# One written order for all engines, one inverse for two chunks and merged key-query products in a delta-rule attention with a softplus feed-forward layer

## The chip, the cores and the metric

One Trainium2 chip, one of its cores, one launch. The metric is the device time of the launch in microseconds (us); the kernel before was run three times: 306.86, 308.31 and 309.32 us, median 308.31 us. One further execution was profiled; every duration below comes from it.

In the profile PE is TensorE (matrix multiply; PEld is its weight load), DVE is VectorE, ACT is ScalarE, POOL is GpSimd and SP is SyncE, which here only issues DMAs.

## The reference, cut to what matters

Batch 4, 8 heads, 768 time steps, head size 48. The attention keeps one 48x48 state for each of the 32 (batch, head) pairs; its output feeds a two-layer network with softplus between.

```python
k_n = k / (np.linalg.norm(k, axis=-1, keepdims=True) + 1e-06)
for t in range(S):
    readout = np.einsum('bhd,bhde->bhe', q[:, :, t], state)
    y[:, :, t] = g[:, :, t] * readout
    v_old = np.einsum('bhde,bhd->bhe', state, kt)
    state = state + bt[:, :, :, None] * np.einsum('bhd,bhe->bhde', kt, vt - v_old)
...
h = x @ w_in                                            # 3072 x 384 by 384 x 2048
g = np.maximum(h, 0.0) + np.log1p(np.exp(-np.abs(h)))   # softplus
return (g @ w_out).astype(np.float32)                   # by 2048 x 384
```

Each state depends on the one before it. The kernel gets rid of the loop over t by chunks of 64 steps: within a chunk the updates solve a triangular system, whose inverse it computes for all heads at once; between chunks the state is carried.

## The kernel before, in words

**Tiling.** Time is cut into 12 chunks of 64 steps. A tile has 128 partitions: 64 time steps of two batches. All 12 chunks pass through the same items (the names are those of the code's `add` calls):

- `load` (line 344): k, q, v, g of a chunk, two DMAs of 192 KB for each, all issued on SP in one chain. `wload` (line 371): eight DMAs for the two weight matrices, issued on POOL.
- `front` (line 468): `cast` k and q to fp16; `trs`, 16 PE transposes (line 485); `kev`, copies from PSUM; `gramk`, 64 matmuls of the keys with themselves (lines 522 and 527); `kkc`, their negated copies into `kk`; `gramq`, 32 matmuls of keys with queries (line 561); `mask` (line 571).
- `norms` and `lane_beta` (lines 410 and 455): `ksq` (ACT), `red` (DVE), the root (ACT for the first chunks, `pow` on POOL later, line 443), `eps`, and `lbeta`.
- `inverse` (line 584): `ln`, a DVE transpose that brings each 32x32 block into one partition (line 591); `diag`, `prep` and 15 `step`s of two instructions each (lines 622 and 629), a forward substitution on 16x16 blocks; transposes back, `tn` and `t32` (lines 647 and 663), which land in fp32 tiles and are rearranged and cast by ACT (lines 654 and 670); then PE products that join the 16 blocks to 32 and prepare 64: `xmm`, `tmm` and `zmm`, with the copies `xs`, `td2` and `z`.
- `chain` (line 765), the part that carries the state: `ks` (keys by state), `w` (v minus it), `umm` (64 matmuls of 32x32 for a chunk, line 840), `u1`, `zu`, `u2`, `smm` and `s` (the new state), `qs` and `ymm` (readout), `y` (times g), `ytr` and `xt` (transposes for the network). `vs` scales v by the key norm on POOL (line 808).
- `dense` (line 998), the network: `g1` (line 1014), `soft` (softplus on ACT, line 1028), `g2` (line 1044), `o` (eviction) and `store`. Chunks 0, 1, 10 and 11 are done alone, with 256 columns in a `g1` matmul, the others in pairs, with 512.

**Two chunks in one inverse.** The lanes of a tile hold 32 blocks of two chunks. Chunks 0 and 1 have an inverse each, chunk 0 on DVE and chunk 1 on POOL; the other five inverses take two chunks each and run on POOL: seven in all.

**What sets the order.** Each item gets an engine and a priority from a table of words (`_TABLE`, line 1108). `Plan.run` (line 86) places the items by estimated costs: on each engine, among the items that are ready, the one with the lowest priority. That gives each engine a fixed program when the kernel is built. Among its costs is one for PE's instructions: `BLOCK` 128 matmuls and `FETCH` 3.5 (lines 49 and 50).

**Buffers.** Every tile comes from a ring of buffers: five PSUM banks for all small products (`d`), two for `g1` (`h`), one for `g2` (`o`); k has 3 buffers, q 2, v and g 4 each.

**Start.** DVE clears the padding of `kn` and `qn` (line 238). POOL issues the eight loads of beta, and clears `kk`, `nv` and `tt` (lines 272 and 275).

Of the kernel before, what the change touches and what calls it, by code (L numbers as in the profile page):

```python
# [16 lines left out]
class Ring:  # L17

    def __init__(self, tiles, ordered=True):
        self.free = [(0.0, i) for i in range(len(tiles))]
        self.tiles = tiles
        self.ordered = ordered
        self.made = self.given = 0


class Buf:
    def __init__(self, ring):
        self.ring = ring  # L30
        self.users = 0
        self.ap = None
        self.slot = None
        self.done = 0.0
        self.no = ring.made
        ring.made += 1


class Item:
    __slots__ = (  # L40
        "eng", "kind", "cost", "fn", "deps", "bufs", "prio", "start", "end", "tail", "n",
        "order", "mm", "mode", "leave", "dma", "after", "tag", "alt",
    )


class Plan:


    BLOCK = 128
    FETCH = 3.5  # L50
    HOP = 0.08
    SWITCH = 0.1
    STAY = 15
    LOOK = 0.15

    def __init__(self):
        self.items = []
        self.tag = None

    def add(  # L60
        self, eng, kind, cost, fn, deps=(), bufs=(), prio=0, tail=None, order=(), mm=0,
        mode=None, leave=None, dma=0.0, after=0.0, alt=None,
    ):
        it = Item()
        it.eng, it.kind, it.cost, it.fn = eng, kind, cost, fn
        it.deps = [d for d in deps if d is not None]
        it.order = [d for d in order if d is not None]
        it.bufs, it.prio = list(bufs), prio
        it.tail = (0.17 if eng == "PE" else 0.0) if tail is None else tail
        it.start = it.end = None  # L70
        it.n = len(self.items)
        it.mm, it.mode, it.leave, it.dma, it.after = mm, mode, leave or mode, dma, after
        it.tag, it.alt = self.tag, alt
        for b in it.bufs:
            b.users += 1
        self.items.append(it)
        return it

    def use(self, table):

        for it, word in zip(self.items, table.split()):
            en = {"P": "PE", "D": "DVE", "A": "ACT", "G": "POOL", "S": "SP"}[word[0]]
            it.cost = it.alt[en] if it.alt else it.cost
            it.eng, it.prio = en, int(word[1:])

    def run(self):
        left = {e: [] for e in ("PE", "ACT", "DVE", "POOL", "SP")}
        for it in self.items:
            left[it.eng].append(it)
        free = {e: 0.0 for e in left}  # L90
        pipe = 0.0
        mode = None
        issued, arrive = 0, [0.0, 0.0]
        done = []
        while any(left.values()):
            best = None
            for e, lst in left.items():
                cands = []
                for it in lst:
                    if any(d.end is None for d in it.order) or any(  # L100
                        d.end is None for d in it.deps
                    ):
                        continue
                    ready = it.after
                    for d in it.deps:
                        t = d.end + (d.tail + self.HOP if d.eng != e else 0.0)
                        ready = max(ready, t)
                    need = {}
                    for b in it.bufs:
                        if b.ap is None:  # L110
                            need[b.ring] = need.get(b.ring, 0) + 1
                    ok = True
                    for r, n in need.items():
                        if n > len(r.free) or (
                            r.ordered
                            and any(
                                b.no >= r.given + n
                                for b in it.bufs
                                if b.ring is r and b.ap is None
                            )  # L120
                        ):
                            ok = False
                            break
                        ready = max(ready, sorted(r.free)[n - 1][0])
                    if ok:
                        cands.append((ready, it))
                if not cands:
                    continue
                t0 = max(free[e], min(r for r, _ in cands))
                at = {it.n: max(t0, r) for r, it in cands}  # L130
                can = [it for r, it in cands if r <= t0 + self.LOOK]
                if e == "PE":

                    def late(it):
                        last = (issued + it.mm - 1) // self.BLOCK
                        at = arrive[min(last, len(arrive) - 1)]
                        return max(0.0, at - t0 - it.cost)

                    stall = min(late(it) for it in can)
                    can = [it for it in can if late(it) <= stall + 0.3]  # L140
                if e == "PE":
                    it = min(can, key=lambda x: (x.prio - self.STAY * (x.mode == mode), x.n))
                else:
                    it = min(can, key=lambda x: (x.prio, x.n))
                t0 = at[it.n]
                if best is None or t0 < best[0]:
                    best = (t0, e, it)
            if best is None:
                raise RuntimeError("no item can be placed")
            t0, e, it = best  # L150
            left[e].remove(it)
            for b in it.bufs:
                if b.ap is None:
                    b.ring.free.sort()
                    b.slot = b.ring.free.pop(0)[1]
                    b.ap = b.ring.tiles[b.slot]
                    b.ring.given += 1
            it.fn(it.eng) if it.alt else it.fn()
            it.start = t0
            if it.dma:  # L160
                free[e] = t0 + it.cost if e == "POOL" else max(t0 + it.cost, pipe - 4.0)
                pipe = max(pipe, t0 + it.cost) + it.dma
                it.end = pipe + 1.9
            elif e == "PE":
                if it.mode != mode:
                    t0 += self.SWITCH
                mode = it.leave
                end = t0 + it.cost
                block = issued // self.BLOCK
                issued += it.mm  # L170
                while issued // self.BLOCK > block:
                    block += 1
                    end = max(end, arrive[block])
                    arrive.append(end + self.FETCH)
# [1037 lines left out]
```

## Time and profile before

| | |
|---|---|
| median of three runs (lowest to highest) | 308.31 us (306.86 to 309.32) |
| profiled execution: span from first to last instruction | 307.5 us |
| PE busy, matmuls | 236.3 us, 6768 |
| DVE, ACT and POOL busy | 158.9, 142.9 and 142.6 us |
| first `g1` | 72.83 us after the start |
| first `g1` of 512 columns, that is of chunks 2 and 3 | 121.33 us |
| last matmul ends | 303.3 us |
| mean granted TensorE clock | 0.967 of full speed |

The profiled execution's own span lies 0.8 us under the median. Busy times of the engines overlap, since all run at once; a matmul's duration in a group is also longer than what it adds, since matmuls are pipelined. "issue" is time in which an engine waited for nothing that the profile shows. The strips of the page cut the span into 40 slices of 7.7 us, and each digit is a tenth.

### The profile page before, as it was taken

The numbers are of one execution on the slowest core, as the hardware profiler recorded it, in microseconds if no ns is written. First come the engines' busy times: TensorE is split into PE (matmuls) and PEld (weight loads), VectorE is DVE, ScalarE is ACT, GpSimd is POOL, SyncE is SP. The second block draws the span as 40 slices with busy tenths as digits, with TensorE's granted clock in tenths as the row PEclk, the third lists the DMA queues.
The fourth block names the chain that finished last, engine by engine and source line by source line (L and its number), as shares of the span: only waits on it lengthen the run. The fifth ranks groups of instructions, "written<-read, shape, count | busy, mean of one in ns | idle before, by whom it ended". The sixth has DMA issues, their size and how long they took to land.

```text
span 307.5 us, 14779 instructions
## 1 busy us (share of the span) xinstructions
PE 236.3 (77%) x6768; PEld 155.8 (51%) x6768; DVE 158.9 (52%) x306; ACT 142.9 (46%) x240; POOL 142.6 (46%) x262
## 2 busy tenths in 40 slices
PE   0130183277988997899987999959999899999993
PEld 0120163255756765455664556636555555567761
DVE  1189998442757786854873474645436611152000
ACT  3070086022754656726654674352656516715531
POOL 8916578557138887457761747811087000000000
PEclk9999999999999999969997999987999979999999
DMA  8999439999015979699298430843000111021122
GB/s 115 158 179 173 57 54 191 186 170 152 7 31 100 157 140 158 113 162 148 51 164 147 83 57 15 125 99 79 6 5 15 43 28 30 2 55 28 27 53 51
DMA packets 107711, 27.79 MB, mean 90 GB/s; under 512 B 100865, under 2 KB 107649, under 8 KB 107649
## 3 DMA queue, kind: packets, MB, share of 16 engines
q1 hardware_dynamic: 103680, 23.60, 47.5%
q0 software_dynamic: 3968, 3.25, 7.1%
q8 instruction: 53, 0.87, 1.2%
q14 instruction: 10, 0.07, 0.1%
HBM read 25.26 MB, written 4.72 MB: 98 GB/s over the span
## 4 chain that ended last, share of the span: by engine, by line
PE 61%; DVE 12%; issue 11%; POOL 11%; ACT 4%; POOLq 0%; ACTq 0%
PE h L1014 19%; PE o L1044 18%; PE d L485 3%; POOL tt L629 3%; POOL tmp L622 3%; PE d L684 2%; PE d L786 2%; DVE tt L629 2%; PE d L840 2%; PE d L939 2%; DVE tmp L622 2%; PE d L711 2%; DVE ln L591 2%; PE d L561 2%; PE d L877 2%
## 5 line engine op out<-in xcount | busy, mean ns | idle before, releaser
L1044 PE MATMUL o<-w_out,ga 128*128 128x384 f16 x384 | 77.9, 343 | 3.2 <-issue 1.9
L1028 ACT ACTIVATE ga<-h 128x512 f16<-128x512 f32 x96 | 57.2, 599 | 48.0 <-PE h L1014 45.4
L1014 PE MATMUL h<-xt,w_in 128*128 128x512 f16 (+1 forms) x384 | 74.8, 336 | 1.0 <-issue 1.0
L1044 PEld LDWEIGHTS <-ga 128*128 128x128 f16 x384 | 35.7, 101 | 26.1 <-issue 7.3
L1014 PEld LDWEIGHTS <-w_in 128*128 128x128 f16 x384 | 36.1, 100 | 21.7 <-issue 3.4
L629 POOL TENSOR_TENSOR tt<-tt,tmp 128x30 f32<-128x30 f32 (+7 forms) x90 | 33.8, 375 | 7.0
L622 POOL TENSOR_TENSOR tmp<-nn,tt 128x30 f32<-128x30 f32 (+7 forms) x90 | 32.3, 359 | 6.4
L485 PE MATMUL d<-ident,kn 128*128 128x128 f16 x96 | 9.7, 258 | 30.8 <-POOL kn L314 28.3
L312 ACT ACTIVATE kqt<-d 128x512 f16<-128x512 f16 x26 | 15.0, 596 | 26.2 <-PE d L485 24.5
L314 DVE CAST u<-d 128x384 f16<-128x384 f32 x25 | 13.4, 552 | 26.3 <-PE d L877 18.5
L443 POOL TENSOR_TENSOR nv<-nv,half_c 128x32 f32<-128x32 f32 x4 | 22.0, 5509 | 7.4 <-DVE nv L423 7.4
L485 PEld LDWEIGHTS <-kn 128*128 128x128 f16 x96 | 7.1, 115 | 32.8 <-POOL kn L314 28.7
L571 DVE TENSOR_TENSOR mt<-d,mask 128x512 f16<-128x512 f32 x24 | 15.7, 683 | 9.9 <-PE d L561 9.8
L808 POOL TENSOR_TENSOR vf<-vf,nv 128x768 f32<-128x768 f32 x11 | 16.2, 1476 | 8.2 <-DMA vf<-in_v_dram 5.0
L314 DVE COPY osb<-o 128x384 f32<-128x384 f32 x12 | 6.6, 551 | 22.7 <-PE o L1044 22.7
L961 DVE TENSOR_TENSOR yg<-d,gf 128x384 f16<-128x384 f32 x24 | 12.8, 551 | 10.1 <-PE d L939 10.0
L654 ACT CAST tn<-tn 128x512 f16<-128x512 f32 (+1 forms) x7 | 6.7, 963 | 21.6 <-DVE tn L647 21.6
L314 DVE COPY kqt<-d 128x512 f16<-128x512 f16 x22 | 9.1, 422 | 14.6 <-ACT kqt L312 9.0
L423 DVE TENSOR_REDUCE nv<-ksq 128x16 f32<-128x768 f32 x12 | 11.4, 949 | 9.6 <-POOL nv L275 7.8
L312 ACT ACTIVATE u<-d 128x384 f16<-128x384 f32 x23 | 10.7, 490 | 10.7 <-PE d L840 7.4
L829 DVE TENSOR_TENSOR w<-vf,d 128x384 f16<-128x384 f32 x22 | 11.3, 547 | 8.2 <-PE d L786 4.5
L591 DVE STREAM_TRANSPOSE ln<-kk 128x1024 f16<-128x1024 f16 x7 | 13.3, 1905 | 4.2 <-ACT kk L312 4.0
(89 smaller groups left out, 379.4 us busy)
## 6 DMA issues: line engine op xcount, KB each, us to landing
kf<-in_k_dram SPq DMA_DIRECT2D x24, 192.0 KB, 5.4
vf<-in_v_dram SPq DMA_DIRECT2D x24, 192.0 KB, 5.5
qf<-in_q_dram SPq DMA_DIRECT2D x24, 192.0 KB, 5.5
gf<-in_g_dram SPq DMA_DIRECT2D x24, 192.0 KB, 5.3
out_dram<-osb SPq DMA_DIRECT2D x48, 96.0 KB, 2.3
w_in<-in_moe_w_in_dram POOLq DMA_DIRECT2D x4, 384.0 KB, 8.1
w_out<-in_moe_w_out_dram POOLq DMA_DIRECT2D x4, 384.0 KB, 8.6
beta_l<-in_beta_dram POOLq DMA_DIRECT2D x8, 12.0 KB, 4.5
```

Source lines behind the costliest of these rows:

```text
L312: nc.scalar.activation(o, x, AF.Copy, scale=float(sign))
L314: ENG[en].tensor_copy(o, x)
L443: lambda: nc.gpsimd.tensor_tensor(nv.ap[:, sl], nv.ap[:, sl], half_c[:, sl], ALU.pow),
L485: nc.tensor.transpose(o[:, NP * p + i], x.ap[:, p, 2 * i : 2 * i + 2].rearrange("p h d -> p (h d)"), ident,)
L571: nc.vector.tensor_tensor(o.ap, gm[m].ap.rearrange("p (n t) -> p n t", n=H), mask[:, None, :].broadcast_to([P, H, C]), ALU.mult,)
L591: lambda: nc.vector.transpose(ln.ap, kk.ap[:, 1].rearrange("p u t -> p t u")),
L622: eng.tensor_tensor(t, nn.ap[:, :, j + 1 :, j : j + 1].broadcast_to([P, 2, n, w]), tt.ap[:, :, j : j + 1, 16 : 16 + w].broadcast_to([P, 2, ...
L629: eng.tensor_tensor(rows, rows, t, ALU.add)
L808: nc.gpsimd.tensor_tensor(vf.ap, vf.ap, nv.ap[:, 16 * cl : 16 * cl + 16] .rearrange("p (a h) -> p a h", a=2)[:, :, :, None] .broadcast_to( ...
L1014: nc.tensor.matmul(hp.ap[:, n * b : n * b + n], w_in[:, j, f * P : (f + 1) * P], xt.ap[:, j, t0 : t0 + n], start=(j == 0), stop=(j == 2),)
L1028: lambda hp=hp, o=gb: nc.scalar.activation(o.ap, hp.ap, AF.Softplus),
L1044: nc.tensor.matmul(op.ap[:, :DM], b.ap[:, col + c0 : col + c0 + 128], w_out[:, f, :], start=(f == 0), stop=(f == NF - 1),)
```

## The change

- **Order.** `Plan` with its costs and priorities is gone. `Program.emit` walks one list of 1,227 words, `_ORDER`, each an engine's letter and an item's number, and writes the items in that order. As before, an engine carries out its own items strictly in the order in which they were written.
- **Inverse.** Chunks 0 and 1 share one inverse on DVE. Six inverses instead of seven; the other five stay on POOL.
- **fp16 transposes in place.** `step` leaves its result in a smaller fp32 tile. A new item, `c16`, copies it as fp16 into a zeroed tile; `tn` and `t32` then transpose fp16 straight into their final tiles, with the rearrangement in the transpose's own write pattern. The two ACT casts are gone.
- **Merged products.** From chunk 2 on `gramk` and `gramq` become one `gram`: 64 matmuls of 128 columns for a chunk instead of 64 of 64 and 32 of 64. It comes in two halves (p = 0, 1), each with its own two PSUM banks, and `kkc` and `mask` with it: four pieces of 256 elements a partition instead of two of 512.
- **Solve.** `umm` multiplies only one half of the 32-row blocks and copies the other half through an identity: 36 matmuls for a chunk instead of 64. `z` carries an identity in its first half, so `zu` takes 64 rows at once.
- **Start.** The memsets of `kk`, `nv` and `tt` on POOL are gone. DVE zeroes two `tw` tiles, writes ten strips of `kqt` and the identities of four `z` tiles. The second halves of the first two k loads are issued on ACT, the first halves on SP; chunk 1's k goes first.
- **Halves.** In chunks 0 and 1 casts and transposes go by halves; in all chunks `ks`, `qs` and `smm` go by halves. Four of the twelve `vs` move to DVE. k gets a fourth buffer, `kn` a fifth, `g` loses one.

The matmuls of all items come to 6112 in the new order, against 6768.

```diff
-    def run(self):
-        left = {e: [] for e in ("PE", "ACT", "DVE", "POOL", "SP")}
...
+    def emit(self, table):
+        done = set()
+        for word in table.split():
+            en, no = word[0], int(word[1:])
+            it = self.items[no]
...
+            it.fn(en)
...
-    r_kk = ring("kk", 2, [P, 2, U, HC], F16, init=pool0)
-    r_nv = ring("nv", 3, [P, 32], F32, init=lambda t: nc.gpsimd.memset(t, 1.0))
-    r_t = ring("tt", 2, [P, 2, 16, 48], F32, init=pool0)
...
+    for t in r_t16.tiles:
+        nc.vector.memset(t, 0.0)
+    for t in r_kqt.tiles:
+        nc.vector.memset(t[:, 4 * NP * C :], 0.0)
...
+    for t in r_z.tiles:
+        nc.vector.tensor_copy(t[:, :, :HC], pat[:, None, :].broadcast_to([P, 16, HC]))
...
+                                nc.tensor.matmul(o[QUAD[2 * r], i], x[:, :HC], x)
+                                nc.tensor.matmul(o[QUAD[2 * r + 1], i], x[:, HC:C], y)
...
+        c16 = add("c16", tag, "DAG", lambda en: copy(en, tw.ap[:, :, :, 16:32], tt.ap),
+                  deps=[prev], bufs=[tt, tw])
+        tn_it = add("tn", tag, "D",
+                    lambda en: nc.vector.transpose(
+                        tn.ap.rearrange("p u j -> p j u"),
+                        tw.ap[:, :, :, 16:32].rearrange("p b i j -> p j (b i)"),
+                    ),
...
+            def t32(en, b=b):
+                c0 = 16 - 16 * b
+                nc.vector.transpose(
+                    td.ap.rearrange("p u i -> p i u")[:, 16 * b : 16 * b + 16],
+                    tw.ap[:, b, :, c0 : c0 + 32],
+                )
...
+            def umm(en, m=m, up=up, w1=w1):
+                o = hd(up.ap)
+                for r in range(2):
+                    f = QUAD[2 * r + 1]
+                    nc.tensor.matmul(o[f], ident[f, f], w1.ap[f])
+                for pi in range(H):
+                    for r in range(2):
+                        f = QUAD[2 * r]
+                        nc.tensor.matmul(
+                            o[f, pi], td.ap[f, 16 * cl + 2 * pi + m, :], w1.ap[f, pi]
+                        )
...
-    plan.use(_TABLE)
-    plan.run()
...
+    prog.emit(_ORDER)
```

In the new order the items that matter here come so, with the matmuls written up to there: first `xmm` after 208 matmuls, first `g1` after 750, the last `gram` of chunks 2 and 3 after 1033, first `g1` of 512 columns after 2172. POOL's words between the third and fourth of these: the second inverse (chunks 2 and 3), `pow` for chunks 4 and 5, `vs` of chunk 2, a cast, `vs` of chunk 3.

## The prediction

> **What bounds the kernel now.** I read the strips of the page first, then busy time by stage, then the chain of waits in the stage where PE starves.
>
> ```profile
> PE   0130183277988997899987999959999899999993
> DMA  8999439999015979699298430843000111021122
> ```
>
> PE is nearly empty for eight slices (62 us) and nearly full from the eleventh on, so the kernel is a long start and then a PE-bound stretch. By stage, in the busy times of three stretches, cut at the first `g1` (72.83) and at the first `g1` of 512 columns, chunks 2 and 3 (here 125.64, its third; the first is at 121.33); columns are length, then busy time and instructions of each engine, granted clock, DMA share, GB/s:
>
> ```profile
> 0.00:72.90 72.90, 23.27 (x1019) 18.36 (x1020) 44.97 (x97) 22.68 (x41) 48.45 (x102) 1.00 1.02 142
> 72.90:125.64 52.74, 47.25 (x1491) 34.27 (x1492) 36.01 (x64) 30.94 (x50) 34.41 (x50) 1.00 0.63 106
> 125.64:303.30 177.66, 165.75 (x4260) 103.20 (x4258) 77.93 (x146) 88.80 (x150) 59.71 (x112) 0.94 0.36 65
> ```
>
> PE is 32%, 90% and 93% busy. The first stretch holds most of what can be won. Its beginning, by time of start, duration, engine and line:
>
> ```profile
> 6.75 3.55 POOL L272 MEMSET kk<- 128x2048 f16 x2
> 10.42 2.69 POOL L272 MEMSET tt<- 128x1536 f32 x2
> 13.17 0.82 POOL L314 CAST kn<-kf 128x768 f16<-128x768 f32 x1
> ...
> 24.41 0.16 DVE L622 TENSOR_TENSOR tmp<-nn,tt 128x30 f32<-128x30 f32 x1
> ...
> 37.29 1.03 DVE L647 STREAM_TRANSPOSE tn<-tt 128x512 f32<-128x512 f32 x1
> ```
>
> The first k landed at 6.10 (ACT's wait for it ends there), but its cast comes behind POOL's memsets at 13.17. The inverse of chunk 0 then takes DVE from 24.41 to 37.29, 12.9 us. In the chain of waits from 40 to 73 us, "issue" is 39.6%, in these pieces (start, length):
>
> ```profile
> 47.10 1.60 issue
> ...
> 52.09 3.08 issue
> ...
> 57.37 4.26 issue
> ...
> 65.39 1.35 issue
> ...
> 70.12 1.99 issue
> ```
>
> Counting PE's matmuls up to each stop gives 479, 607, 735, 863 and 991: exactly 128 apart, 256 instructions with their weight loads. The queue table agrees:
>
> ```profile
> q8 instruction: 53, 0.87, 1.2%
> ```
>
> 53 packets of 16.4 KB, and 6768/128 is 52.9. PE waits for its own instructions. The stops end at 48.70, 55.17, 61.63, 66.74 and 72.11, so a block took 6.5, 6.5, 5.1 and 5.4 us, with the DMA engines full (share 1 to 1.4).
>
> **What the Trainium skill says.** "Runtime: NRT & Kernel Launch", section "Instruction fetch mechanics", has blocks of 16 KiB or 256 instructions, as counted here, but calls the fetch hidden; the trace differs, 12.3 us of stops. "TensorEngine Tiling (Array Packing)", section "Key Properties", says that changing the tiling mode drains PE; no row of the trace shows that alone, so its price is inside my mean for a small matmul below. "VectorE: DVE Perf Modes", section "The TRN2 errata", gives `120 + FD` cycles of 0.96 GHz for a PSUM source, so 0.39 us for 256 elements: pieces of half the size cost more than half. The rows agree (0.551 us for 384, 0.683 for 512: 0.42 by the slope).
>
> **The change part by part.**
>
> *PE work.* At the end of the trace 12 `g1` matmuls of 256 columns take 1.31 us and four `g2` 0.65, six `g1` of 512 take 1.29. The network: 192 x 0.109 + 192 x 0.215 + 384 x 0.163 = 124.8 us, 129.1 at the mean clock 0.967. The other 6000 matmuls have the remaining 107.2 of 236.3 us: 17.9 ns each. The change takes away 10 x 32 (merged `gram`) and 12 x 28 (`umm`), leaving 5344 small ones: 95.7 us, total 225, 12 less. Bounds: nothing saved on `gram` (its columns only move: 64x64 + 32x64 before, 64x128 after), so 6 less, to 15 less.
>
> *Other engines.* ACT loses the rearranging casts to `td` and `tn` (12.1 + 6.7 us) and gains about as much: five more casts of 0.84 and 30 `kkc` of 0.39 instead of 14 of 0.60 among them; the new words with the old durations sum to 142 us, as before. POOL loses one inverse, 13 us (30 instructions from 186.65 to 199.78), 6.5 of memsets and three `vs` of 1.48 (11 to 8), and gains a cast: about 125 from 143. DVE gains: `mask` 4 x 0.68 + 40 x 0.42 = 19.5 instead of 16.4; `kkc` 18 x 0.42 = 7.6 instead of 6.7; four `vs` of some 1.0 (768 elements; `red` over as many takes 0.95); five `c16` of 0.4 and four clears of 0.5; 4 more of setup; less one inverse's transposes, 1.9 + 1.05 + 1.35 = 4.3. That is 12 to 20 more, 171 to 179 from 159. It hides behind PE as long as PE is full; between 51 and 100 DVE has some 42 us to do in 49, which is the place where it would show, with up to the 12 to 20. The fp16 transposes aren't in the trace in this form; nearest are `ln` (1.86 ns an element, fp16, strided read), `tn` (2.05) and `t32` (1.3). I take 1.05 us for `tn` and 0.85 for a `t32`; from 0.7 to 2 us each.
>
> *Start.* k of chunk 1 is issued on SP at 0.8 and on ACT behind the table load, which with its activation ends at 2.30; the first pair landed 4.4 us after its second issue, so 6.7. Behind the two issues on ACT (0.85 each, SP's spacing) only the first casts are queued, and they wait for the same k. By then DVE is through its memsets (7 x 0.165, about 1.4 for `tw`, 0.8 for `kqt`, 1.5 for `z`, from 1.64): 6.5. Then half casts (0.33), `trs` 0.65, `kev` 0.42, `gramk` 0.5, `kkc` 0.42 for four halves, interleaved with `ksq` (0.84) and `red` (0.95) twice, `sqrt`, `eps`, `lbeta` (1.0): `ln` at 13.4 instead of 20.0. `ln` 1.9, `prep` 0.8, 12.9 of steps, `c16` 0.4, `tn` 1.05: first `xmm` at 30.5, where before `tn` ended at 38.3. The loads queued on SP (1.4 us each) deliver k and q of chunks 2 and 3 by about 32; weights are issued on POOL at 25 to 32, 8.1 to landing: covered.
>
> *Instructions.* The first `xmm` comes after 208 matmuls; the stops will stand at the same counts, 223 + 128n. The loads still saturate the DMA engines to about 60 us (loads have 47.5% of the span, weights 7.1%, all moved forward). With 5.0 us a block (between 3.5, the constant `FETCH` that the kernel before plans with, and the 6.5 of the longest): 351 at 35.6, 479 at 40.6, 607 at 45.6, 735 at 50.6, 863 at 55.6, 991 at 60.6. The first `g1` (750) is at 51, 22 sooner. The last `gram` of chunks 2 and 3 (1033) is at 61.5; `kkc` and `ln` 2.5; POOL's `prep` and steps 14.4 (185.37 to 199.78): the second inverse ends at 78.4, against 74.4 before. Behind it on POOL stand `pow` (5.5) and `vs` (1.48), on which `w` of chunk 2 waits; on DVE `eps` for chunk 4 waits for that `pow`, with an `o` behind it. Then two chains: `w` 0.55, `umm` 0.65, `u1` 0.55, `zu` 0.4, `u2` 0.55, `smm` 0.6, `s` 1.1, `ks` 0.4, and again to `y`, `ytr`, `xt` 5.2: 10; hops and one block 5. `g1` of chunk 2 starts at 78.4 + 7 + 10 + 5 = 100, against 121.33. Up to there PE has the network of chunks 0 and 1 (21 us) and small work (20) in 49 us: it fits.
>
> *Rest.* From there 104.7 us of network (108.2 at the clock) and 3392 small matmuls (60.7): 168.9. Before, PE took 177.66 for 165.75, 93.3%; I take 95.5%, since 10% fewer blocks are fetched (48 instead of 53) and one wait for an inverse is gone: 176.9. At 93.3% it would be 181, at 97% 174. From the last matmul to the end 4.2, as before. 100 + 176.9 + 4.2 = 281.1; the median lay 0.8 above the span: 282.
>
> **The rivals.**
>
> *Tighter* (24%). Instructions come in 3.5 to 4 us a block, so the second inverse ends at 71: `g1` of chunk 2 at 92, then 96.5%: 92 + 175 + 5 = 272, down to 262. For it: the kernel's own 3.5. Against: full DMA engines until 60.
>
> *Looser* (12%). Blocks take 6.5 us and bunched `xmm`, `tmm` (264 matmuls in a row, two blocks) stop PE in each inverse; `g1` of chunk 2 at 107, then 91%: 107 + 185.6 + 5 = 298. For it: the longest stops stand before the products of the inverse. Against: only 60 us are so loaded.
>
> *Slower* (6%). The strided fp16 write of `tn` and `t32`, 1536 elements an inverse. It lies bare on the path in the first two inverses; in the other four some 10 us of POOL's slack cover it. With x more an inverse, 2x + 4(x - 10) = 26 at x = 11, 7 ns an element on top of about 2: from 9 ns, five times `ln`, the time passes 308; at x = 12 it is 314. Against: no transpose in the trace needs over 2.05.
>
> *The change doesn't bear* (4%): the start is won, and the same stops and waits give it back, 308.
>
> **How the numbers follow.** The forecast has 54%, 282, alone 275 to 290. With 24 and 12 for the neighbours I leave out the last few of each: 266 to 298. Faster by over 1% (about what this measurement can tell) 90%, within 1% 4%, slower 6%.
>
> **What would show it.** Right: `ln` near 13 to 14, `xmm` near 30, first `g1` near 51, stops of PE 128 matmuls apart to 65 us, about 48 instruction packets, `g1` of 512 columns near 100, PE at 95% after it. Wrong: `tn` or `t32` over 3 us; PE idle behind DVE after 100; `g1` of chunk 2 after 115; no stops at all (then the tighter rival).

## The result, and the profile after

| | before | after | forecast |
|---|---|---|---|
| median of 20 runs each (lowest to highest) | 308.53 us (304.84 to 311.49) | 306.2 us (301.31 to 311.14) | 282 |
| after to before, 95% interval | | 0.988 (0.983 to 0.993) | 0.915 |
| profiled execution, span | 307.5 us | 304.6 us | 281.1 |
| PE busy, mean granted clock | 236.3 us, 0.967 | 241.7 us, 0.943 | 225 |
| DVE, ACT, POOL busy | 158.9, 142.9, 142.6 us | 184.7, 131.4, 120.5 us | 171 to 179, 142, 125 |
| first `g1`; first `g1` of 512 columns | 72.83; 121.33 us | 52.16; 111.99 us | 51; 100 |

Faster by 1.2%, where 8.5% was forecast. (Ratios, here and below, leave disturbed runs out, so they can differ from the quotient of the medians, by up to 1.3 points.) The strips of the page, in slices of 7.6 us:

```profile
PE   1432347789959996869877999969899969999993
PEclk9999999999969999799985799995999988999999
DMA  9999999999900197983979521341035110002113
```

Of the first eight slices seven stood at 0 to 3 tenths in before, and six stand at 1 to 4 now; but in the stretch of nines there are more sixes, sevens and eights. By stage, cut at the first `g1` and at the first `g1` of 512 columns (columns: length, then busy time and instructions of PE, PEld, DVE, ACT, POOL, granted clock, DMA share, GB/s):

```profile
0.00:52.16 52.16, 20.12 (x751) 16.08 (x751) 39.47 (x100) 18.72 (x37) 19.78 (x35) 1.00 1.07 152
52.16:112.00 59.84, 52.24 (x1427) 38.74 (x1423) 41.25 (x77) 29.17 (x56) 32.14 (x61) 0.94 0.71 102
112.00:300.40 188.40, 169.34 (x3949) 106.00 (x3940) 103.97 (x171) 83.02 (x157) 68.56 (x125) 0.93 0.40 71
```

The first stretch is 21 us shorter. The last holds the PE work that was forecast for it (169.3 against 168.9 us), but PE is 90% busy in it instead of 95.5%. It stands idle for 18.9 us there (11.9 in before, from its own first `g1` of 512 columns on): 11.8 us end with something of VectorE's, `tn`, a mask or `td` (1.2 in before), and 6.2 us are waits for its own instructions (9.9 in before).

Measured by finished network matmuls, after is 7% of them ahead at 80 us (11% against 4%), 5% at 100, 1% at 140, and behind at 160 (33% against 34%): the start is won, and lost between 100 and 160 us.

Two traces can only be compared from a common point. The changed kernel and three runs below that are the same up to there (`e4`, `e14`, `e16`) reach the first `g1` at 52.2 to 56.5 us, with 7.9 to 13.8 us of stops for instructions ahead of it; the changed kernel's own trace has the least.

DVE's groups of the page (last columns: count, busy us and mean ns, idle time ahead) and two waits (us in all, times, longest) say where to look:

```profile
L534 DVE STREAM_TRANSPOSE td<-tw 128x512 f16<-128x512 f16 x12 | 28.7, 2452 | 0.0
L524 DVE STREAM_TRANSPOSE tn<-tw 128x512 f16<-128x512 f16 x6 | 14.3, 2377 | 2.6 <-POOL tw L200 2.4
```

```profile
PE d L555 <- DVE tn L524: 13.3, 5, 3.6
PE d L576 <- DVE td L534: 2.5, 2, 2.2
```

`tn` takes 2.38 us and a `t32` 2.45, where 1.05 and 0.85 were forecast. PE, in its fixed order, stands in front of `xmm` until `tn` is there, five times, 13.3 us in all; in before that happened with 3.5 us in all.

### The profile page after: what moved, and what is told of

It is laid out like the page before. It is cut to its first block, busy times and chain, and to the rows that moved or that the text cites. A ratio compares the mean times of both kernels' runs of the same rounds, so it can differ in the third digit from the quotient of the medians.

```text
span 304.6 us, 13469 instructions
## 1 busy us (share of the span) xinstructions
PE 241.7 (79%) x6112; PEld 160.8 (53%) x6112; DVE 184.7 (61%) x348; ACT 131.4 (43%) x250; POOL 120.5 (40%) x219
## 4 chain that ended last, share of the span: by engine, by line
PE 46%; DVE 21%; POOL 17%; issue 10%; ACT 3%; DMA 2%; DVEq 0%; POOLq 0%; ACTq 0%
PE h L825 14%; PE o L852 14%; POOL tmp L504 8%; POOL tt L511 7%; DVE td L534 4%; DVE tn L524 3%; DVE ln L481 3%; PE d L649 3%; DMA kf<-in_k_dram 2%; PE d L715 2%; DVE tt L511 2%; PE d L289 2%; POOL nn L496 2%; DVE tmp L504 2%; PE d L765 1%
## 5 line engine op out<-in xcount | busy, mean ns | idle before, releaser
L825 PE MATMUL h<-xt,w_in 128*128 128x512 f16 (+1 forms) x384 | 82.0, 352 | 0.0
L511 POOL TENSOR_TENSOR tt<-tt,tmp 128x30 f32<-128x30 f32 (+7 forms) x75 | 27.7, 369 | 5.9
L534 DVE STREAM_TRANSPOSE td<-tw 128x512 f16<-128x512 f16 x12 | 28.7, 2452 | 0.0
L414 DVE TENSOR_TENSOR mt<-d,mask 128x256 f16<-128x256 f32 x40 | 16.8, 435 | 9.8 <-ACT kk L198 6.7
L555 PE MATMUL d<-tn,kk 16*32 16x16 f16 x768 | 7.3, 173 | 16.8 <-DVE tn L524 13.3
L198 ACT ACTIVATE osb<-o 128x384 f32<-128x384 f32 x14 | 6.9, 492 | 27.2 <-PE o L852 26.9
L496 POOL TENSOR_TENSOR nn<-ln,bl 128x256 f32<-128x256 f16 x10 | 6.3, 650 | 30.9 <-DVE ln L481 30.9
L649 PE MATMUL d<-s,kqt 48*64 48x48 f16 x704 | 16.7, 192 | 1.7 <-issue 1.4
L649 PEld LDWEIGHTS <-kqt 48*64 48x64 f16 x704 | 13.5, 112 | 8.4 <-issue 7.7
L555 PEld LDWEIGHTS <-kk 16*32 16x32 f16 x768 | 7.1, 93 | 18.8 <-issue 15.2
L657 POOL TENSOR_TENSOR vf<-vf,nv 128x768 f32<-128x768 f32 x8 | 11.8, 1472 | 13.2 <-DMA vf<-in_v_dram 13.2
L780 DVE TENSOR_TENSOR yg<-d,gf 128x384 f16<-128x384 f32 x24 | 12.8, 551 | 5.7 <-PE d L765 5.6
```

The costliest lines, as they stand in the source:

```text
L198: nc.scalar.activation(o, x, AF.Copy, scale=float(sign))
L414: nc.vector.tensor_tensor(mt[c][m].ap[:, NP * p : NP * p + NP], gb[m].ap.rearrange("p (n b) -> p n b", n=NP)[:, :, C:], mask[:, None, :].b ...
L511: eng.tensor_tensor(rows, rows, t, ALU.add)
L534: nc.vector.transpose(td.ap.rearrange("p u i -> p i u")[:, 16 * b : 16 * b + 16], tw.ap[:, b, :, c0 : c0 + 32],)
L555: nc.tensor.matmul(uv(xp.ap)[QUAD[qd], u], kk.ap[r, 0, u, :], tn.ap[r, u, :])
L649: nc.tensor.matmul(hd(o.ap)[HALF[r], NP * p + i], kq_of(c, p)[FEAT[m], 2 * i + r, off : off + C], s0[r].ap[FEAT[m], NP * p + i], **start(p ...
```

## The experiments

Every kernel ran beside the kernel before on the same chip. All ratios are to the kernel before, with a 95% interval; the changed kernel itself has 0.988. "Mended" means `e7_whole_then_copy`.

| run | median us | ratio |
|---|---|---|
| `e1_fp32_and_casts` | 311.5 | 0.992 (0.987 to 0.997) |
| `e2_rows_written_whole` | 304.1 | 0.982 (0.976 to 0.988) |
| `e3_busy_work` | 308.7 | 0.997 (0.993 to 1.001) |
| `e4_order_only` | 323.1 | 1.042 (1.035 to 1.049) |
| `e5_four_quadrants` | 307.9 | 0.994 (0.988 to 1.000) |
| `e6_before_in_place` | 329.9 | 1.074 (1.067 to 1.081) |
| `e7_whole_then_copy` | 295.1 | 0.960 (0.954 to 0.967) |
| `e8_both` | 298.0 | 0.967 (0.959 to 0.975) |
| `e9_tn_alone` | 300.4 | 0.976 (0.967 to 0.985) |
| `e10_td_alone` | 302.5 | 0.982 (0.971 to 0.992) |
| `e11_idle_transposes` | 298.7 | 0.971 (0.963 to 0.979) |
| `e12_busy_work_again` | 302.2 | 0.980 (0.970 to 0.991) |
| `e13_narrow_g2` | 294.0 | 0.957 (0.950 to 0.964) |
| `e14_narrow_g2_unmended` | 301.7 | 0.987 (0.979 to 0.995) |
| `e15_td_by_scalar` | 301.2 | 0.982 (0.974 to 0.990) |
| `e16_ln_ahead` | 306.1 | 1.000 (0.995 to 1.004) |
| `e17_mended_ln_ahead` | 296.1 | 0.959 (0.953 to 0.966) |

### The transposes

**Undo them.** `tw` in fp32; the transposes contiguous, into tiles that are free by then; the casts on ScalarE.

```diff
-  nc.vector.transpose(tn.ap.rearrange("p u j -> p j u"), ...)
+  nc.vector.transpose(flat(nn), ...)
+  nc.scalar.copy(tn.ap, flat(nn).rearrange("p j u -> p u j"))
```

> The changed kernel with one part undone: the three transposes at the end of each inverse go to contiguous fp32 tiles again, and ScalarE casts and rearranges them. Theory 1 (the slow strided fp16 transposes make tn and td late, TensorE stands in front of xmm and then runs at half clock): tn comes 0.43 + 1.04 + 1.09 + a hop = 2.7 us after the last step instead of 0.43 + 2.38 = 2.8, so the stops in front of xmm stay near 3 us; td comes 1.4 us earlier per inverse, the wait of tmm for it goes, and the time is 302 to 306. Rival 3 (VectorE's load is what costs: 185 us busy): VectorE loses 6 x 4.7 = 28 us, ScalarE gains 18, and the time is 290 to 298. Rival 1 (the place of xmm in the order is what costs): no change, 306.

0.992: no gain. VectorE is 24 us less busy (160.8), so its load alone doesn't set the time. But this run doesn't compare the two forms cleanly: the casts stand in ScalarE's order where this order has no room for them, and PE waits behind them:

```profile
PE d L563 <- ACT tn L531: 11.6, 4, 3.7
PE d L359 <- ACT kqt L198: 8.1, 1, 8.1
```

**Write whole rows, read with a stride.**

```diff
-    r_tn = ring("tn", 2, [P, U, 16], F16)
+    r_tn = ring("tn", 2, [P, 16, U], F16)
-    r_td = ring("td", 3, [P, U, HC], F16)
+    r_td = ring("td", 3, [P, HC, U], F16)
```

> The changed kernel with the fp16 transposes written contiguously (tn as partition, j, u and td as partition, i, u), TensorE reading them with a stride instead. If the stride of the write is what makes them slow, tn takes 1.0 to 1.1 us and each t32 0.7 to 0.9; if it is the two-byte type, they stay at 2.4. Theory 1: tn is 1.3 us and td 4 us earlier per inverse, the stops in front of xmm shrink from 3 to some 1.5 us, fewer of them are followed by half clock, and the time is 293 to 300. Rival 1 (order): the stops shrink by as much, but what stands behind is late for other reasons, 303 to 306. If TensorE's strided reading costs as much per matmul as the write did, xmm, tmm, zmm and umm take over 30 ns each instead of 10 and the time is over 310.

The stride of the write it is: `tn` takes 1.45 us, a `t32` 0.69, with the same type and the same input. But PE pays for reading `td` with a stride. Its groups in the changed kernel, then in this one:

```profile
L694 PE MATMUL d<-w,td 32*32 32x48 f16 x384 | 8.8, 187 | 2.8 <-issue 2.8
L611 PE MATMUL d<-td,kk 32*32 32x32 f16 x384 | 8.2, 176 | 2.2 <-issue 2.2
L608 PE MATMUL d<-td,ident 32*32 32x512 f16 x24 | 5.5, 455 | 0.0
```

```profile
L695 PE MATMUL d<-w,td 32*32 32x48 f16 x384 | 14.4, 216 | 4.5 <-issue 4.5
L612 PE MATMUL d<-td,kk 32*32 32x32 f16 x384 | 14.9, 229 | 0.1
L608 PE MATMUL d<-td,ident 32*32 32x512 f16 x24 | 12.6, 1038 | 0.0
```

512 moving columns at a stride of 64 bytes take 1.04 us instead of 0.46. In all PE is busy for 253.2 us, 11.5 more than in the changed kernel, and the time is no longer for it. `xmm`, reading `tn` so, costs only 8.0 instead of 7.3 us. That suggested the next version.

**Whole rows, then a copy for `td`.**

```diff
-  nc.vector.transpose(td.ap.rearrange("p u i -> p i u")[:, 16 * b : 16 * b + 16], ...)
+  nc.vector.transpose(tds, ...)
+  nc.vector.tensor_copy(td.ap[:, :, 16 * b : 16 * b + 16], tds.rearrange("p i u -> p u i"))
```

> The changed kernel with tn written contiguously and read with a stride by xmm (which cost 0.7 us in all in the run that did so), and td transposed contiguously into a scratch tile and copied from there to td by VectorE, so that TensorE reads td as before. Theory 1 (late tn and td): tn 1.45 instead of 2.38, a t32 with its copy 0.7 + 0.5 = 1.2 instead of 2.4, so tn is 0.9 us and td 3.3 us earlier per inverse and VectorE's busy time falls by some 19 us, with no more work on TensorE: 296 to 302. If a strided copy of two bytes is as slow as the strided transpose (0.7 + 2.4 each), td is late again and the time is 304 to 308. Rival (the time is set by TensorE's work and the instruction stops): 304 to 307.

0.960: 2.8 points come back, some 9 us. The copy takes 0.69 us: it reads with a stride of 64 bytes and writes runs of 16 neighbours. No run has a copy that writes single elements 64 bytes apart, so it isn't shown whether a copy would be as slow at that as the transpose. One of the two at a time:

> The changed kernel with tn alone written contiguously (1.45 us instead of 2.38, read with a stride by xmm); td is still transposed in place with a stride, 2.45 us for each half. The version with both mended took 0.960 of the kernel before, the changed kernel 0.988. If the late tn is what costs, nearly all of that comes back here: 0.960 to 0.968 (296 to 299). If the late td is, little does: 0.982 to 0.990 (302 to 305).

> The changed kernel with td alone mended: each half transposed contiguously (0.70 us) and copied (0.69), in place of 2.45; tn is still transposed in place, 2.38 us. If the late td or VectorE's load is what costs, most comes back here: 0.960 to 0.970 (296 to 299), with the wait of tmm for td and the half clock from 156 to 172 us gone and the stops in front of xmm still near 3 us. If the late tn is, 0.980 to 0.990.

0.976 and 0.982: each brings a part, `tn` some 1.2 points and `td` 0.6, against 2.8 together; the intervals are too wide to tell which is the greater.

**The same transposes in the kernel before,** its order kept item by item:

> The kernel before with one part of the change alone: a cast to fp16 on VectorE and strided fp16 transposes straight into tn and td in place of contiguous fp32 transposes and ScalarE's rearranging casts; its order of work is the same, item by item. tn comes 0.43 + 2.38 = 2.8 us after the last step instead of 1.04 + 1.09 = 2.1, td 4.8 us after that cast instead of 1.34 + 1.94 = 3.3; VectorE has 5.2 us more per inverse (seven of them), ScalarE 3 us less. Theory 1: slower, 311 to 318. If the place of the work hides it: 307 to 310.

Slower by 7.4%, 22 us, more than expected. VectorE is busy 192.8 us instead of 158.9:

```profile
L666 DVE STREAM_TRANSPOSE td<-tw 128x512 f16<-128x512 f16 x14 | 32.5, 2503 | 0.1
L656 DVE STREAM_TRANSPOSE tn<-tw 128x512 f16<-128x512 f16 x7 | 16.7, 2384 | 0.1
```

Some 2.6 us of the 22 are not the transposes': here GpSimd clears the two `tw` tiles ahead of its first cast of k (2.69 us), and the first `ln` comes at 22.65 instead of 20.02; in the change VectorE clears them. So this part costs some 6% by itself in the kernel before, and its mending gives back 2.8 points in the new order; the rest of the change more than pays for it (0.988 against 1.074).

### VectorE's load or lateness

A useless strided transpose behind the second copy to `td` of every inverse, in the mended version:

> The version with tn and td mended, and one useless strided transpose of 2.4 us on VectorE behind the second copy to td of each inverse, into the scratch tile: VectorE is as busy as in the changed kernel (184 to 186 us), but tn and td are as early as in the mended one. If lateness of tn and td is what costs, the time stays at 0.960 to 0.968 of the kernel before (295 to 298). If it is VectorE's load (what stands behind the transposes on VectorE: w, u, y, s, mask), it goes back to 0.980 to 0.990 (301 to 305).

0.971 against 0.960, with intervals that overlap: VectorE's load may cost a point, but not the 2.8. With the copies to `td` on ScalarE, one of 1.9 us ahead of `tmm`:

> The version with tn and td mended, the two copies into td on VectorE (0.69 us each, 8.3 us in all) replaced by one on ScalarE (some 1 to 1.9 us, just ahead of tmm), so td is as late as before or 0.5 us later. If VectorE's load is what is left, 290 to 294; if only lateness counts, 295 to 297; if ScalarE, waiting there in its order, holds back the softplus and the evictions behind it, 298 to 304.

0.982: slower than on VectorE, near the last of the three theories in time. What the trace shows is a late `td`: PE waits for this copy three times, 3.3 us in all, 2.5 of them in the last inverse, where the copy stands behind softplus in ScalarE's order. So the run doesn't separate load from lateness.

### The half clock

After each stop of more than 2.5 us in front of `xmm`, from the second inverse on, the granted clock is at half for a while. "TensorE: Matmul & The Clock Gate", section "What's actually happening", of the Trainium skill says that the array's clock falls to half after an idle window of about 3.4 us; here a stop of 2.55 us is long enough. Behind the stops that end at 86.89 (3.56 us) and 122.48 (2.55 us), in the changed kernel (columns: length, PE busy, clock, DMA share, GB/s):

```profile
88.00:93.00 5.00, 5.00 (x30) 0.54 0.00 0
...
124.00:128.00 4.00, 3.37 (x69) 0.66 1.31 143
```

Dummies, useless matmuls in front of the first `xmm` of each inverse from the second on, are to fill the stop:

```diff
+  for _ in range(12):
+      nc.tensor.matmul(xp.ap, ident, warm)
```

> The changed kernel with twelve useless matmuls of 512 columns (2.6 us at full clock) ahead of xmm in the inverses 2 to 6, written to the PSUM buffer that xmm then overwrites; nothing is taken away. If the stop of 2.5 to 3.5 us in front of xmm is what halves the clock, the clock stays at 1.00 through the 4 us behind it, 2 us are won at each of five places, and at the longest patch of half clock (157 to 172 us) up to 7: 295 to 302. If the clock follows something else, TensorE has up to 5 x 2.6 us more to do only where the stops were shorter: 306 to 310.

```profile
88.00:92.00 4.00, 3.28 (x142) 1.00 0.01 4
...
124.00:128.00 4.00, 3.53 (x187) 1.00 1.42 159
```

The clock stays up there, the mean rises from 0.943 to 0.970, and nothing is won: 0.997. The second inverse can be read cleanly, since `xmm` follows `tn` as closely there with the dummies as without them. The sixteen `g2` behind it take 2.77 us instead of 5.00. But then PE stands 1.90 us for instructions, and the first `g1` of 512 columns starts 27.5 us behind the start of `tn` in both kernels. Over the whole run PE's waits for VectorE fall from 27.5 to 16.4 us, and those for instructions rise from 16.9 to 26.1 (some 4 of that ahead of the first `g1`, where one more memset is all that sets the kernels apart). In the fourth and fifth inverses the dummies themselves hold `xmm` up, by 2.8 and 4.1 us more, so the total is no clean price of the half clock. In the mended version:

> The version with tn and td mended, with sixteen useless matmuls of 256 columns (1.7 us at full clock) ahead of xmm in the inverses 2, 3, 5 and 6, where it still waits 2.0 to 2.4 us for tn. If the half clock behind those stops costs time, the mean clock rises from 0.96 to 0.98 and the time falls by 3 to 6 us, to 289 to 292. If what follows a stop has slack enough to hide the half clock, or the useless work only moves it, the time stays at 294 to 298.

0.980, slower than without; the mean clock didn't rise (0.947 against 0.959), so this run says nothing of the clock. Where the gain could be followed, behind the second inverse, a stop for instructions took it; what the half clock costs in the whole kernel stays open.

### PE's work

The prediction took 12 us of PE work off. Giving every instant to the matmul that started last, the timeline shows what became of it:

| PE us | before | after |
|---|---|---|
| `gramk`, `gramq`, `gram` | 15.2 | 11.9 |
| `umm` | 8.1 | 6.6 |
| `ks`, `qs` | 9.3 | 12.8 |
| `smm` | 4.1 | 6.4 |
| `zu` | 6.8 | 8.5 |
| all small matmuls | 96.0 | 97.3 |
| `g1`, `g2` | 140.4 | 144.4 |

`ks`, `qs` and `smm` were split by head parity in the change. 32 neighbours in four quadrants of the array became 16 in two, and a matmul takes 12.8 / 704 = 18.2 instead of 13.2 ns (`smm`, 352, 18.2 instead of 11.6; the expectation's figures for one matmul divide by counts that are too high, its sums hold). Put back:

```diff
-                for r in range(2):
+                for m in range(2):
+                    for r in range(2):
```

> The changed kernel with the inner loops of ks, qs and smm put back as the kernel before has them: one run of 32 matmuls over both head parities, so that neighbours fall into four quadrants of the array, where the change issues two runs of 16 that fall into two; eight words of the order move by one to five places for the PSUM buffers. Theory 2 (the PE work that the prediction took off is not off, because this split gives it back): ks and qs fall from 15.8 to 11.0 ns of TensorE time each (704 of them, 3.4 us) and smm from 16.2 to 10.1 (352, 2.1 us); some 5.5 us less TensorE work, and 301 to 304 if TensorE's own work sets the end. Rival (TensorE waits, its work doesn't count): 305 to 308, with the idle time grown by what the work lost.

`ks` and `qs` fall to 9.4 us, `smm` to 4.4, PE's busy time to 235.2; the ratio is 0.994. Joined to the mended version:

> The two versions before in one: four quadrants for ks, qs and smm, tn written contiguously, td transposed contiguously and copied. Theories 1 and 2 together: what each wins adds up, 291 to 298. If they win the same idle time: no better than the better one alone.

0.967: no better than mended alone. Both runs also join each pair of half steps into one, which has to wait for the inputs of both, so they don't price the quadrants alone. The next run takes work off with every instruction in its place: 360 `g2` matmuls are narrower, and leave most of the sum out of the last 64 columns of the output.

> The version with tn and td mended, with 360 of the 384 g2 matmuls made narrower, 320 columns instead of 384 (the last 64 columns of every output keep the first of their sixteen partial sums): 360 x 64/384 x 0.178 us = 10.7 us of TensorE work less, spread evenly, no instruction fewer and no order changed. The prediction took 12 us of TensorE work off at full price. If TensorE's work counts one for one, 283 to 286 here; if the stops and waits take it up, as they took up the 6 us that the four quadrants saved, 291 to 295; in between if some stretches are bound by it and others not.

0.957 against 0.960: 1 us, where 10.7 us would be 3.5 points. PE's busy time falls by 6.9 us (237.0 to 230.1; part of the 10.7 goes to a lower clock). Where it went stands in PE's timeline, last bracket: idle time ahead and its releaser; first the mended version, then this one:

```profile
85.34 1.20 PE L556 MATMUL d<-tn,kk 16*32 16x16 f16 x128 [2.43 <-DVE tn L525]
...
124.80 0.31 PE L583 MATMUL d<-td,xs 32*16 32x16 f16 x24 [0.90 <-issue]
...
236.76 1.19 PE L556 MATMUL d<-tn,kk 16*32 16x16 f16 x128 [1.97 <-DVE tn L525]
```

```profile
84.49 1.21 PE L556 MATMUL d<-tn,kk 16*32 16x16 f16 x128 [3.36 <-DVE tn L525]
...
124.57 0.31 PE L583 MATMUL d<-td,xs 32*16 32x16 f16 x24 [2.61 <-issue]
...
235.76 0.41 PE L556 MATMUL d<-tn,kk 16*32 16x16 f16 x33 [3.38 <-DVE tn L525]
```

PE comes to the same stops earlier and waits longer, for `tn` or, in the middle line of each, for its next block of instructions. The last `tn` starts at 234.26 instead of 235.25; behind it, where PE is 96% busy, the rest takes 51.5 instead of 54.1 us to the last matmul's end. In this pair PE's work counts one for one only there, in the last 54 us. In the changed kernel itself:

> The changed kernel itself with the same 360 narrower g2 matmuls (the same partial sums left out of the last 64 columns): 10.7 us of TensorE work less. If TensorE's work counts one for one, 295 to 297; if late tn and td set the time, 302 to 306.

0.987 against 0.988: no gain beyond the intervals, which are almost a point wide to each side. Two signs speak for a part of it: the quotients of the medians are 0.974 and 0.992, and from the first `g1` (56.37) to the last `tn` the trace takes 3.4 us less than the changed kernel's, and 2.5 less behind it. So up to about half of the work may have counted here; all of it did not.

### The order

If PE only stands in the wrong place, `xmm` can go behind the ready network matmuls that follow it:

> The changed kernel with its order alone changed: in the inverses 2 to 6 xmm is put behind some 3.2 us of network matmuls that stood right behind it, and tmm so that 1.4 to 2 us of other work lie between them; no instruction is added, removed or changed. Rival 1 (the place in the order costs): the five stops in front of xmm (13.3 us in sum) go, the clock stays up behind them, and the time is 288 to 296. Theory 1 in its strict form (the late tn itself costs, because the recurrence behind it is the path): what is won on TensorE comes back as waits in front of umm and zu, 302 to 307.

Slower, 1.042, in part for a third reason that neither expected. In this order ScalarE comes to a cast for the next chunks 7.66 us before the mask that it waits for, and this mask stands behind the slow transposes; PE's next `g1` waits for ScalarE's softplus (7.47 us at 137.62). The rest of the 17 us by which it is slower than the changed kernel isn't traced. ScalarE's timeline:

```profile
136.70 0.38 ACT L198 ACTIVATE kk<-d 128x256 f16<-128x256 f32 x1 [7.66 <-DVE mt L414]
136.98 0.59 ACT L837 ACTIVATE ga<-h 128x512 f16<-128x512 f32 x1
```

So the run doesn't tell what the place of `xmm` alone is worth; that stays open. The mended version shows another effect of the order. VectorE's timeline behind the third inverse, changed kernel and mended version:

```profile
120.05 2.38 DVE L524 STREAM_TRANSPOSE tn<-tw 128x512 f16<-128x512 f16 x1
122.07 0.61 DVE L414 TENSOR_TENSOR mt<-d,mask 128x256 f16<-128x256 f32 x1
122.59 2.38 DVE L534 STREAM_TRANSPOSE td<-tw 128x512 f16<-128x512 f16 x1
124.60 0.61 DVE L414 TENSOR_TENSOR mt<-d,mask 128x256 f16<-128x256 f32 x1
125.14 2.38 DVE L534 STREAM_TRANSPOSE td<-tw 128x512 f16<-128x512 f16 x1
...
129.10 1.91 DVE L481 STREAM_TRANSPOSE ln<-kk 128x1024 f16<-128x1024 f16 x1 [0.45 <-ACT kk L198]
```

```profile
117.68 1.46 DVE L525 STREAM_TRANSPOSE tn<-tw 128x512 f16<-128x512 f16 x1
...
119.36 0.70 DVE L535 STREAM_TRANSPOSE tds<-tw 128x512 f16<-128x512 f16 x1
120.09 0.59 DVE L536 COPY td<-tds 128x512 f16<-128x512 f16 x1
...
120.93 0.70 DVE L535 STREAM_TRANSPOSE tds<-tw 128x512 f16<-128x512 f16 x1
...
124.35 1.90 DVE L482 STREAM_TRANSPOSE ln<-kk 128x1024 f16<-128x1024 f16 x1 [0.88 <-ACT kk L199]
```

The transposes of one inverse stand in VectorE's queue ahead of `ln`, the start of the next inverse. From `tn` to the next `ln`, in us:

| | 1st | 2nd | 3rd | 4th | 5th | last `tn` at |
|---|---|---|---|---|---|---|
| changed | 39.51 | 17.95 | 9.05 | 36.09 | 24.05 | 245.15 |
| mended | 39.34 | 16.27 | 6.67 | 33.19 | 22.04 | 235.25 |
| narrow `g2` | 38.65 | 16.24 | 6.24 | 32.69 | 21.55 | 234.26 |

From `ln` to its `tn` it is 17.4 to 19.9 us in the first two, and up to 21.0 in the third. So the 9.9 us between the first two at the last `tn` are made, but for 0.9, of 1.7 to 2.9 at each of four places. To test whether this is a loop that sets the time, one place was taken out of it by order alone: the last `gram` of chunks 6 and 7 ahead of `xmm`, and `ln` ahead of both `t32`.

> The changed kernel with its slow transposes, with some twenty words of the order moved at one place: in inverse 3 the last gram of chunks 6 and 7 (PE) goes ahead of xmm, its two casts (ScalarE) behind it, and ln of the next inverse (VectorE) ahead of the two t32 of this one instead of behind them; nothing is added or removed. Theory 3 (until the last inverse the time is set by a loop from tn over VectorE's queue to the next ln, then 17.5 us to the next tn; the strided transposes stand in that queue): ln of inverse 4 comes at 124 to 126 us instead of 129.1, the next tn at 144 to 146 instead of 149.0, what follows is earlier by as much, and the time falls by 3 to 5 us, to 0.973 to 0.980 of the kernel before. If later steps take it up (TensorE's work, the instruction stops): 0.986 to 0.992, with the next tn early and the ln after that at 184 to 186 us as before.

> The version with tn and td mended, with the same words moved. There ln of inverse 4 stands at 124.4 us already, and its norms (pow on GpSimd, 5.5 us behind the inverse before) end near 124 us, so that little is left to win at this place: theory 3 says ln 1 to 2 us earlier, the start of GpSimd's steps 0 to 1 us earlier, and 0.957 to 0.963 of the kernel before (294 to 296 us).

1.000 and 0.959: nothing, in both. `ln` came 6.8 us earlier (122.26), GpSimd's steps only 3.3 (it waits for `lbeta` and the clearing of `tt`, 4.70 us in the first line), and `tn` 1.6, because the cast ahead of it now stands behind `y` and `s` of the chain on VectorE:

```profile
129.22 0.24 POOL L488 COPY tt<-bl 128x32 f32<-128x32 f32 x1 [4.70 <-DVE tt L486]
```

```profile
145.99 1.01 DVE L750 TENSOR_TENSOR s<-s,d 128x384 f16<-128x384 f16 x2
146.91 0.42 DVE L200 CAST tw<-tt 128x512 f16<-128x512 f32 x1
147.37 2.40 DVE L524 STREAM_TRANSPOSE tn<-tw 128x512 f16<-128x512 f16 x1
```

The next `ln` then came 0.9 us earlier. So the loop is not the one thing that sets the time: what was won at this place of it, the next queues took back.

## Why the prediction was wrong

The span missed the forecast by 23.5 us (304.6 against 281.1): 12.0 ahead of the first `g1` of 512 columns, 11.5 between it and the last matmul.

**Start: right, with some luck.** `ln` 13.84 (13.4), first `xmm` 29.95 (30.5), first `g1` 52.16 (51). The luck is in the last: the stop at 351 ended 1.7 us before its forecast (33.9 against 35.6), and the blocks behind it each took about 1 us more.

**Instructions: the place right, the size short.** The stops stand at exactly 351, 479, 607, 735, 863 and 991 matmuls, ending at 33.9 to 64.3 us; 47 packets (48). In the chain of waits:

```profile
43.18 2.28 issue
...
50.26 1.39 issue
...
56.21 2.18 issue
```

A block took (64.3 - 33.9) / 5 = 6.1 us, not 5.0; the rival "looser" had 6.5. So the last `gram` of chunks 2 and 3 ends at 65.1 instead of 61.5; with 1.9 more for `kkc`, `ln` and the steps the second inverse ends at 83.96 instead of 78.4. From there to the first `g1` of 512 columns it was 28.0 instead of 21.6 us. `w` comes 9.6 us after the inverse instead of 7: in VectorE's order it stands behind an `o` eviction, which waits for sixteen `g2` behind `xmm`, and these for `tn`. From `w` on it is 18.5 instead of 15, not traced further. 112 instead of 100.

**Other engines: the term that was mis-sized.** "I take 1.05 us for `tn` and 0.85 for a `t32`; from 0.7 to 2 us each." They took 2.38 and 2.45, 4.65 ns an element: 43.0 us instead of 6 x 1.05 + 12 x 0.85 = 16.5, above the upper bound. The nearest rows were taken for their type and element count, but their writes are contiguous, and that was the one thing new. VectorE as a whole stayed nearer the forecast, 184.7, because its other additions were overpriced. The rival "slower" named the very mechanism; its price of 9 ns was the point from which it would decide alone. With the measured 4.5 us more an inverse its sum gives 2 x 4.5 = 9 us, and 9 us is what the mending brought, but that agreement is luck. It put the loss into the first two inverses and let some 10 us of GpSimd's slack cover the other four; the table above shows 0.2 us behind the first inverse and 1.7 to 2.9 behind each of the next four. GpSimd had its slack, since it waits 30.9 us for `ln` in four inverses; the way to that `ln` leads over VectorE's queue. Worth: 2.8 points, some 9 of the 24 us.

**PE work: wrong, but it hardly mattered.** Removing 656 matmuls took off 4.8 us (`gram` 3.3 of a forecast 5.7, `umm` 1.5 of 6.0). `umm`'s were cheap ones, 8.1 / 768 = 10.5 ns, not the mean of 17.9, and `gram` only moves its columns, which the lower bound had in view. The halves of `ks`, `qs` and `smm`, named in the change and given no price, put 5.8 back. "TensorE: Matmul & The Clock Gate", section "The mechanism", of the Trainium skill says that a weight load runs beside a matmul only in another row group. That would fit `ks` and `qs`, of which each half stays in one row group, but not `smm`, whose halves go back and forth between two and slowed down as much; no run here isolates it.

**Rest: the step that failed.** "168.9 us of PE work at 95.5%": the work was 169.3, the share 90%, and so the stretch took 188.4 us instead of 176.9. The reasons given were fewer blocks and one wait for an inverse less. The waits for instructions did fall, from 9.9 to 6.2 us. But the sum put the waits behind VectorE at nothing, since its load "hides behind PE as long as PE is full", and they rose from 1.2 to 11.8 us. The mended version has 6.4 of them, and its stretch takes 179.7 us: 8.7 of the 11.5 are back. Behind this stands a wrong picture, a stretch in which PE is 93% busy taken for one that PE bounds. With the narrow `g2` PE reaches the same stops sooner and most of the work taken off doesn't count, up to the last `tn`. In these two written orders PE's share is what the queues leave it. Of the rivals, "the change doesn't bear", given 4%, came closest in time and in words: the start is won, and stops and waits give it back. "Looser" had the share, 91%, but for stops that the new `xmm` and `tmm` would make; the stops for instructions didn't grow.

**What stays open.** The mended version stands at 0.960, 296 us beside a before of 308.5 and 14 above the forecast. In its trace 9.7 us of this stand ahead of the first `g1` of 512 columns (109.67 instead of 100) and only 2.8 behind it, so what is left is mostly the opening: slower blocks of instructions and the long way from the second inverse to that `g1`. No run takes the stops for instructions away, so their price is read from where they stand and not tested. On top of the mending, less PE work gave 1 us and one `ln` moved ahead nothing; the price of the half clock and of the place of `xmm` is open.

## What to carry to other kernels

Price a new write pattern by a row that has this pattern, not by type and size; where there is none, keep the contiguous form or put the upper bound well above the nearest row. A busy share of 90% doesn't make an engine the bound when all engines run in written orders: ask which queue each wait ends in, and test by taking work off with every instruction and the order left in place. A step moved ahead is worth only what the next in-order queue lets through. Before a filler is called useless or useful, look at where it ran past the wait that it was to fill.

## What was not expected of the hardware

- A VectorE transpose of 128x512 fp16: 0.69 us with rows read and written whole, 1.45 with a strided read, 2.38 to 2.45 with a strided write (32 or 64 bytes between elements). "VectorE: DVE Perf Modes", section "The three transpose paths", of the Trainium skill has 311 ns for a VectorE transpose of 128x128, four times which would be an estimated 1.24 us for this size, and has no price for a stride; the runs show about half of that with whole rows and twice with a strided write.
- PE reading moving data with a stride of 64 bytes: 1.04 us for 512 columns instead of 0.46.
- Short VectorE instructions stretch while GpSimd runs a long one on its side: the last two steps of the first inverse take 0.80 us beside a cast and 1.41 us beside `vs`, instead of some 0.2, and the cast ahead of the last `tn` takes 1.68 us beside `vs` instead of 0.46. No run separates the two engines.
- Useless matmuls in a stop of PE keep the clock at 1.00 behind it (0.54 without them, at 88 us). The kernel wasn't faster for it (0.997): at the place that could be read cleanly, PE then stood 1.90 us for instructions.
- The stops for instructions in the opening, under full DMA engines, vary from trace to trace of the same program part: 7.9 to 13.8 us ahead of the first `g1`.
